# Two rows of w3 loaded ahead of k, a pairwise maximum for batch 0, and a new order for the first third of the list

## The chip, the cores and the metric

The kernel runs on one core of a Trainium2 chip. The metric is device time in microseconds of one launch; for the kernel before it is 227.48 us, the median of 3 runs (227.4 to 227.79).

## The reference

There are eight batches of 8 heads, 576 positions and 64 features. From q, k and v a linear attention is computed, and its output goes through a feed-forward block with a product in place of an activation:

```
q_s = exp(q - max over features); q_s /= sum + 1e-9
k_s = exp(k - max over positions); k_s /= sum + 1e-9
kv  = k_s^T v           (64 x 64 for each head)
x   = q_s kv            (4608 tokens x 512)
out = ((x w1) * (x w2)) w3 w_out
```

Inputs and output are float32; w1 and w2 are 512 x 1024, w3 is 1024 x 1024, w_out 1024 x 512.

## The kernel before, in words

Since nothing nonlinear stands between w3 and w_out, the kernel first multiplies them on chip to one matrix W3O (1024 x 512), and every token then goes through x w1, x w2, their product, and one multiplication with W3O.

**The fold** (`fold(ft)`, L384 to L412). For each of the eight rows ft of w3 (128 x 1024, cast to float16 by its load): `w3t.ft` transposes eight 128 x 128 blocks on TensorE into a bank of PSUM, `w3T.ft` copies them to SBUF (on ScalarE or VectorE, into one of two buffers), `pf.ft.0` and `pf.ft.1` multiply four blocks each with one half of w_out (`wo.0`, `wo.1`), and `W3O.ft` scales the sum into place.

**Attention** (`attention(b)`, from L417). For q: `qmx` maximum, `qsub` subtraction, `qexp` exponential, `qsm` sum, `qeps` and `qrc` its reciprocal, `qn` scaling. The result is transposed: by TensorE for batch 0 (`qt`, copied by `qT`), by a DMA for the others (`qd`). For k: the maximum over positions is taken in two steps, `kmx` over the nine positions that a partition holds, and `cb` across partitions (two transposes of 32 x 32 blocks and small reductions). Then `ksub` and `kexp`, `kv` (TensorE, k_s^T v), `kv2` (division by the sums), `xm` and `xt` (TensorE, x for 512 and the last 64 positions of the batch) and `xs`, `xts` (copies out of PSUM). For batch 0, k and q are loaded and worked on by pairs of heads (the last number in a name), and `kmx` is one reduction per pair (L426); for the other batches ScalarE copies two positions into PSUM (`kmi`, L433) and VectorE takes maxima of that bank with the rest in SBUF (`kmx_half`, L437).

**Chunks** (`chunk(c)`, from L795). Chunk c is the first 512 positions of batch c; chunk 8 collects the last 64 of all batches. `up.1` and `up.0` are x w2 and x w1 (L809), `bs` copies the first out of PSUM, `ab` is the product, `down` multiplies with W3O (L842), `os` copies out, `st` stores. Later chunks use a variant with fewer products (`um`, `dm` and their additions, with the sums of weights `ws` and `wt`).

**Order.** `ORDER` (L83) is a list of all steps, written out, and `Plan.run` (L52) emits them in this order. A letter behind a slash is the engine (`/A` ScalarE, `/D` VectorE, `/P` GpSimd). Each engine works off its own steps in the order of the list and waits at each for what it needs. The steps `zero.0` to `zero.6` (L302) multiply a tile of zeros and feed nothing; the number behind the slash is the count of 128 x 512 matmuls, and `zero.0` has 13.

**Loads.** q of batch 0 is loaded from SyncE; the weights, and k, v and the other q of batches 0 and 1, from GpSimd, whose queue also runs its own computing steps in the same order (L375). The loads of batches 2 to 7 come from SyncE, and those of batch 2 start when `w1.1` has landed (GATES, L80). VectorE and GpSimd steps marked `port` are made to run one after another where the engine changes (L69).

Of the kernel before, what the change touches and what calls it, by code (L numbers as in the profile page):

```python
# [10 lines left out]
F32 = mybir.dt.float32  # L11
F16 = mybir.dt.float16
AF = mybir.ActivationFunctionType
ALU = mybir.AluOpType
# [69 lines left out]
zero.5/3 zero.0 zero.1/1 q.0.0 qmx.0.0 qsub.0.0/D q.0.1 qmx.0.1 ident w3.3 w3.4 qexp.0.0 w3t.3 w3T.3/A qsm.0.0  # L84
qeps.0.0/D qsub.0.1/D zero.4/3 zero.2/1 w3t.4 zero.3/6 w3T.4/A wo.0 pf.3.0 pf.4.0 qexp.0.1 qrc.0.0 qn.0.0/D qt.0.0.0
qt.0.0.4 qT.0.0.4/A wo.1 pf.3.1 zero.6/1 qsm.0.1 w3.6 w3t.6 qeps.0.1/A qrc.0.1 qT.0.0.0/D qn.0.1/D pf.4.1 W3O.4/D w3.0
w3t.0 W3O.3/D w3T.6/A pf.6.0 qt.0.1.0 w3T.0/A qT.0.1.0/A qt.0.1.4 pf.6.1 qT.0.1.4/A W3O.6/A pf.0.0 k.0.1 kmx.0.1 k.0.0
w3.7 w3t.7 w3T.7/A pf.0.1 w3.5 w3t.5 pf.7.0 pf.7.1 w3T.5/A pf.5.0 w3.1 w3.2 v.0 k.1 kmx.0.0 cb.0 ksub.0.0/D kexp.0.0
w3t.1 w3T.1/D W3O.7/A ksub.0.1/D pf.5.1 w2.1 w2.0 w1.0 q.1.0 W3O.5/D w2.2 w3t.2 pf.1.0 kexp.0.1 pf.1.1 W3O.1/D w1.1
kv.0.0 kv.0 kv2.0 w3T.2/A pf.2.0 kmi.1 kmx.1.0 xm.0.1 xt.0 xs.0.1.1/A xs.0.1.0/A xts.0.0/A xts.0.1/D pf.2.1 W3O.2/A  # L90
xm.0.0 xs.0.0.1/A xs.0.0.0/A q.1.1 up.1.0.1.0 W3O.0/A wt.1/P up.1.0.1.1 up.1.0.0.1 up.1.0.0.0 bs.0.1.1/A up.0.0.0.0
bs.0.0.1/A kmx.1.1 cb.1 bs.0.0.0/A qmx.1.0 up.0.0.0.1 up.0.0.1.0 qsub.1.0/D ksub.1.1/D ab.0.0.1 qexp.1.0 qsm.1.0
up.1.0.0.3 bs.0.0.3/A up.0.0.1.1 ab.0.1.1 q.2 v.1 kexp.1.1 k.2 qeps.1.0/A ksub.1.0/P up.1.0.1.2 kexp.1.0 up.1.0.0.2
qrc.1.0 bs.0.0.2/A qn.1.0/P up.0.0.0.3 up.0.0.0.2 ab.0.0.0 qmx.1.1 qd.1.0 qsub.1.1/P bs.0.1.0/A ab.0.0.3 up.1.0.1.3
up.0.0.1.3 ab.0.0.2 k.3 ab.0.1.0 bs.0.1.3/A ab.0.1.3 ws.1.1/D up.0.0.1.2 bs.0.1.2/A ab.0.1.2 down.0.0.0 qmx.2.0
down.0.0 down.0.1.0 down.0.1 vc.1.1/A vc.1.0/A qexp.1.1 qsm.1.1 qeps.1.1/A ws.1.0/P qsub.2.0/P kv.1.0 kv.1 q.3 kv2.1
qexp.2.0 down.0.2.0 down.0.2 qrc.1.1 xm.1.0 qn.1.1/P qd.1.1 qmx.2.1 down.0.3.0 down.0.3 qsm.2.0 qeps.2.0/D kmi.2
kmx.2.0 qsub.2.1/P xs.1.0.0/A v.2 xs.1.0.1/A up.1.1.0.0 bs.1.0.0/A os.0.2/A st.0.2 up.0.1.0.0 os.0.3/A qrc.2.0
qn.2.0/P wt.2/P up.1.1.0.1 up.0.1.0.1 bs.1.0.1/A qexp.2.1 kmx.2.1 up.1.1.0.2 cb.2 bs.1.0.2/A ksub.2.0/P up.0.1.0.2
up.1.1.0.3 os.0.0/A os.0.1/A xm.1.1 xs.1.1.1/A qsm.2.1 xs.1.1.0/D ab.1.0.1 qeps.2.1/A qrc.2.1 ab.1.0.0 bs.1.0.3/A  # L100
up.0.1.0.3 up.1.1.1.0 up.0.1.1.0 up.1.1.1.1 qmx.3.1 up.0.1.1.1 ab.1.0.3 ab.1.0.2 bs.1.1.0/A up.1.1.1.2 up.0.1.1.2
up.1.1.1.3 qn.2.1/P kexp.2.0 down.1.0.0 down.1.0 kmi.3 kmx.3.0 bs.1.1.1/A ab.1.1.1 vc.2.0/A qd.2.0 xt.1 bs.1.1.2/A
ksub.2.1/P vc.2.1/A kmx.3.1 cbt.3 kexp.2.1 qsub.3.1/P xts.1.0/A ab.1.1.2 xts.1.1/A q.4 qexp.3.1 ws.2.0/P ab.1.1.0 kv.2
kv2.2 down.1.1.0 down.1.1 qd.2.1 xm.2.1 qmx.3.0 qsub.3.0/P os.1.0/A bs.1.1.3/A xs.2.1.1/A qmx.4.1 qsub.4.1/P xm.2.0
xs.2.0.1/A xt.2 qsm.3.1 xs.2.0.0/A xs.2.1.0/A cbx.3 xts.2.1/A v.3 down.1.2.0 up.0.1.1.3 up.1.2.0.0 bs.2.0.0/A qmx.4.0
xts.2.0/D up.0.2.0.0 up.1.2.0.1 qsub.4.0/P up.0.2.0.1 up.1.2.0.2 k.4 v.4 qexp.3.0 cb.3 ksub.3.1/P qsm.3.0 os.1.1/A
up.0.2.0.2 ab.1.1.3 up.1.2.0.3 q.5 qeps.3.1/A qrc.3.1 qn.3.1/P bs.2.0.1/A st.1.0 qexp.4.1 qsm.4.1 bs.2.0.2/A ab.2.0.2
ab.2.0.1 qexp.4.0 kmi.4 up.0.2.0.3 up.1.2.0.4 up.0.2.0.4 qeps.3.0/A kmx.4.0 qrc.3.0 vc.3.1/A bs.2.0.3/A ab.2.0.3
qn.3.0/P ab.2.0.0 bs.2.0.4/A kexp.3.1 up.1.2.0.5 up.0.2.0.5 q.6 qsm.4.0 bs.2.0.5/A ab.2.0.5 up.1.2.0.6 qeps.4.1/A
st.0.3 qd.3.1 kmx.4.1 down.1.2 qrc.4.1 ab.2.0.4 down.1.3.0 up.0.2.0.6 up.1.2.0.7 up.0.2.0.7 qd.3.0 os.1.2/A down.1.3  # L110
bs.2.0.6/A qmx.5.0 ab.2.0.6 vc.3.0/A ksub.3.0/P kexp.3.0 st.1.2 qeps.4.0/A bs.2.0.7/A qn.4.1/P os.1.3/A qsub.5.0/P
qrc.4.0 qn.4.0/P cbt.4 cbx.4 kv.3 ab.2.0.7 qexp.5.0 down.2.0 kv2.3 xm.3.0 xs.3.0.1/A xs.3.0.0/A xm.3.1 xs.3.1.0/A xt.3
xts.3.1/A xts.3.0/A cb.4 ksub.4.1/P k.5 qmx.6.1 down.2.1 xs.3.1.1/D qsm.5.0 vc.4.1/A os.2.1/A ksub.4.0/P up.1.3.0.0
up.0.3.0.0 qmx.6.0 qsub.6.0/P bs.3.0.0/A ab.3.0.0 os.2.0/A qeps.5.0/A qrc.5.0 st.1.1 qmx.5.1 qsub.5.1/P up.1.3.0.1
up.0.3.0.1 up.1.3.0.2 up.0.3.0.2 bs.3.0.1/A qd.4.1 up.1.3.0.3 up.0.3.0.3 up.1.3.0.4 ab.3.0.1 v.5 kmi.5 kmx.5.0 kmx.5.1
cbt.5 st.2.1 kexp.4.0 vc.4.0/A kexp.4.1 kv.4 bs.3.0.2/A qsub.6.1/P kv2.4 bs.3.0.4/A up.0.3.0.4 ab.3.0.4 down.2.2
bs.3.0.3/A ab.3.0.2 qexp.5.1 qd.4.0 cbx.5 qsm.5.1 qexp.6.0 xm.4.1 xs.4.1.0/A xm.4.0 xs.4.0.1/A qn.5.0/P xs.4.0.0/A
up.1.3.0.5 ws.3.1/D up.0.3.0.5 up.1.3.0.6 up.0.3.0.6 v.6 qeps.5.1/A wt.4/D ws.4.0/D os.2.2/A wt.3/D ws.3.0/D qrc.5.1
qn.5.1/P qexp.6.1 cb.5 ksub.5.0/P bs.3.0.6/A ab.3.0.6 k.6 vc.5.0/A xs.4.1.1/A up.1.3.0.7 up.0.3.0.7 q.7 qsm.6.1
ab.3.0.3 bs.3.0.5/A vc.6.0/A up.1.4.0.0 ab.3.0.5 up.0.4.0.0 up.1.4.0.1 st.1.3 bs.3.0.7/A ksub.5.1/P up.0.4.0.1 qsm.6.0  # L120
kmi.6 bs.4.0.1/A bs.4.0.0/A kmx.6.0 st.2.0 vc.6.1/A down.2.3 qeps.6.1/A os.2.3/A qrc.6.1 kmx.6.1 up.1.4.0.2 qd.5.0
qn.6.1/P qeps.6.0/A qrc.6.0 qn.6.0/P up.0.4.0.2 ab.4.0.0 up.1.4.0.3 bs.4.0.2/A ab.4.0.2 up.0.4.0.3 up.1.4.0.4
up.0.4.0.4 cbt.6 kexp.5.0 bs.4.0.3/A vc.5.1/A qmx.7.0 qsub.7.0/P ab.4.0.3 cbx.6 up.1.4.0.5 ab.4.0.1 cb.6 up.0.4.0.5
ksub.6.1/P bs.4.0.4/A ab.4.0.4 ab.3.0.7 st.0.0 xt.4 kexp.5.1 kv.5 xts.4.0/A qexp.7.0 kv2.5 bs.4.0.5/A ab.4.0.5 dm.3.1
xts.4.1/D dm.3.2 de.3.1/A qd.5.1 xm.5.0 xm.5.1 xs.5.0.1/A xs.5.0.0/A qd.6.0 ad.3.1/D xs.5.1.0/A up.1.4.0.6 up.0.4.0.6
up.1.4.0.7 up.0.4.0.7 xs.5.1.1/A st.0.1 ksub.6.0/D kexp.6.0 ad.3.3/D bs.4.0.6/A dm.3.7 kexp.6.1 bs.4.0.7/A ws.2.1/D
ad.3.2/D dm.3.6 xd.5.3/D de.3.7/A ab.4.0.6 xt.5 ad.3.4/P qmx.7.1 ab.4.0.7 xts.5.1/D kv.6 xts.5.0/A dm.3.4 de.3.2/A
dm.3.5 de.3.4/A kv2.6 dc.3.3 qd.6.1 xm.6.1 xs.6.1.0/A qsub.7.1/P dc.3.1 xd.5.2/P xs.6.1.1/A qsm.7.0 um.5.2.1 um.5.1.1
ue.5.1.1/A ue.5.2.1/A xm.6.0 xd.5.4/D xt.6 xts.6.0/A ad.4.1/D dm.3.3 xts.6.1/A dc.3.2/A um.5.1.6 xd.5.1/D dc.3.4/D
ue.5.1.2/A k.7 xs.6.0.1/A ad.4.2/D um.5.2.6 ue.5.2.2/A ad.4.4/D um.5.1.7 ws.4.1/D um.5.2.7 ue.5.2.7/A um.5.0.7  # L130
um.5.1.5 ue.5.1.4/A ue.5.1.7/A ad.4.3/D um.5.2.2 uc.5.2.1 qeps.7.0/A um.5.0.1 xs.6.0.0/A um.5.2.4 uc.5.2.3 qrc.7.0
ue.5.0.7/A um.5.1.3 uc.5.1.4/P ab.5.1.1 ue.5.0.1/A um.5.2.5 ue.5.2.4/A um.5.1.2 uc.5.1.1 ab.5.2.0/P st.3.0 st.2.2
um.5.0.2 uc.5.0.1 um.5.0.4 um.5.0.6 ue.5.0.2/A uc.5.0.3 uc.5.2.4/P um.5.3.7 xd.6.3/P qn.7.0/P dm.4.1 kmi.7 kmx.7.0
um.5.3.1 ue.5.3.7/A um.5.1.4 uc.5.1.3 ab.5.1.0/P kmx.7.1 ue.5.3.1/A um.5.3.2 uc.5.3.1 de.4.1/A um.5.0.5 ue.5.0.4/A
uc.5.0.4/P um.5.3.6 xd.6.2/P ue.5.3.2/A dm.4.6 um.5.2.3 ab.5.2.1 um.6.0.1 qexp.7.1 qsm.7.1 cbt.7 um.5.3.5 ue.5.3.4/A
dm.4.2 xd.6.1/D dm.4.7 um.6.2.1 um.5.0.3 um.5.3.3 dc.4.1 ab.5.0.1 v.7 vc.7.1/A um.5.3.4 uc.5.3.3 uc.5.3.4/P ab.5.0.0/P
de.4.7/A dm.4.4 st.3.1 qeps.7.1/A qrc.7.1 ue.6.0.1/A ab.5.3.1 um.6.0.6 ab.5.3.0/P um.6.0.7 cbx.7 cb.7 de.4.2/A dc.4.3
xd.6.4/D ue.6.0.2/A ue.6.0.7/A ue.6.2.1/A dm.4.5 de.4.4/A dc.4.4/D um.6.0.5 ue.6.0.4/A uc.6.0.4/D st.4.1 um.6.1.1
ue.6.1.1/A um.6.2.7 ue.6.2.7/A dm.4.3 dc.4.2/A um.6.3.1 ue.6.3.1/A um.6.0.4 um.6.3.7 ue.6.3.7/A um.6.0.2 ksub.7.1/D
ksub.7.0/D qd.7.0 qn.7.1/P kexp.7.1 um.6.1.6 um.6.3.6 um.6.2.6 ue.6.2.2/A uc.6.0.3 uc.6.0.1 ab.6.0.0/P um.6.3.4  # L140
vc.7.0/A um.6.2.4 uc.6.2.3 um.6.0.3 ab.6.0.1 um.6.2.2 uc.6.2.1 um.6.1.2 uc.6.1.1 um.6.1.7 um.6.3.2 uc.6.3.1 ab.6.2.0/P
# [25 lines left out]
def kernel(  # L167
# [11 lines left out]
    nc = tc.nc  # L179
    B, H, S, D = q.shape  # L180
# [81 lines left out]
    OWN = (3, 384)  # L262
    LAST = [0, 256, 384, 512]
    FEXP = []
    CX = [3, 4, 5, 6, 7]
    DH = [0, 1]
    KE = []
    ABX = []
# [108 lines left out]
    for b in range(2, B):  # L377
        for n in "kqv":
            load((n, b), "SP")
# [803 lines left out]
```

## Time and profile before

| what | value |
|---|---|
| median of 3 runs | 227.48 us |
| the profiled execution | 227.57 us |
| its span in the profile | 225.8 us |
| TensorE busy | 219.3 us, 97% |
| VectorE busy | 203.9 us, 90% |
| ScalarE busy | 161.6 us, 72% |
| GpSimd busy | 141.1 us, 62% |

The span is the profiler's time from first to last instruction; the execution's own time is 1.8 us longer. Busy time is the union of an engine's instructions. TensorE's matmuls are pipelined with modelled ends, so the rate is better read from starts: 16 matmuls of 512 columns start within 3.5 us. In the views a row gives start, duration, engine, line, operation and tiles; what stands in brackets is the idle time just before and what ended it.

### The profile page before, as it was taken

To read this page: it belongs to the slowest core of one execution; us is meant where nothing else is said; L and a number is where in the kernel's file an instruction comes from. 1 tells how busy PE (TensorE), PEld (TensorE's weight loads), DVE (VectorE), ACT (ScalarE), POOL (GpSimd) and SP (SyncE) were. 2 spreads that over 40 slices of the span, in tenths; PEclk is the share of its full clock that TensorE was granted. 3 is DMA by queue.
4 is the path that set the end of the run, shared out by engine and by line. 5 is a ranking of instruction groups with operands and counts; after the bars stand their busy time and mean duration, and the time that the engine had idled before them with its cause. 6 is when DMAs were issued, how large, how long until landed. Compare 5 with 4: busy or idle time off the path is not lost.

```text
span 225.8 us, 5662 instructions
## 1 busy us (share of the span) xinstructions
PE 219.3 (97%) x2250; PEld 150.6 (67%) x2250; DVE 203.9 (90%) x363; ACT 161.6 (72%) x280; POOL 141.1 (62%) x96
## 2 busy tenths in 40 slices
PE   7998999999999999999999999999999999999994
PEld 2454658865886544444444657888888888888853
DVE  2989879989998999999998999999999988899881
ACT  2556476785859997899999986988995846453511
POOL 8344405787999799999679928297474055602320
PEclk9999999999999999999999999999999999999999
DMA  6999999999999999999969186482193040044343
GB/s 222 214 273 248 294 227 251 367 387 300 277 276 369 388 324 357 187 312 280 385 164 296 22 134 212 128 221 96 32 200 64 3 107 34 3 124 157 89 145 139
DMA packets 38042, 46.89 MB, mean 208 GB/s; under 512 B 18048, under 2 KB 21504, under 8 KB 38016
## 3 DMA queue, kind: packets, MB, share of 16 engines
q1 hardware_dynamic: 32144, 35.92, 56.5%
q0 software_dynamic: 5728, 10.55, 20.0%
q8 instruction: 17, 0.28, 0.5%
q10 hardware_dynamic: 144, 0.07, 0.1%
q14 instruction: 9, 0.07, 0.1%
HBM read 38.80 MB, written 9.44 MB: 214 GB/s over the span
## 4 chain that ended last, share of the span: by engine, by line
PE 67%; DMA 20%; DVE 8%; ACT 2%; POOL 1%; issue 1%; POOLq 0%; ACTq 0%; SPq 0%; DVEq 0%
PE pab L809 19%; PE uA L904 12%; PE dA L945 8%; DMA w1sb<-in_moe_w_dram 8%; PE uB L904 6%; PE po L842 6%; DMA w<-in_moe_w_dram 5%; DMA wosb<-in_moe_w_out_dram 5%; PE dB L945 4%; DMA q<-in_q_dram 3%; PE uC L904 3%; PE po L857 3%; PE dC L945 2%; DVE qm L547 2%; PE pkv L501 2%; DVE qr L579 2%
## 5 line engine op out<-in xcount | busy, mean ns | idle before, releaser
L809 PE MATMUL pab<-x,w2sb 128*128 128x256 f16 (+1 forms) x224 | 40.6, 318 | 0.0
L809 PE MATMUL pab<-x,w1sb 128*128 128x256 f16 (+1 forms) x224 | 40.6, 318 | 0.0
L597 POOL TENSOR_TENSOR en<-eq,qr 128x1024 f16<-128x1024 f16 (+1 forms) x14 | 29.7, 2126 | 8.3 <-DVE k L475 4.3
L809 PEld LDWEIGHTS <-w2sb 128*128 128x128 f16 x224 | 21.6, 98 | 13.4 <-issue 1.0
L809 PEld LDWEIGHTS <-w1sb 128*128 128x128 f16 x224 | 21.7, 98 | 13.0 <-issue 0.2
L553 POOL TENSOR_TENSOR q<-q,qm 128x1280 f32<-128x1280 f32 (+1 forms) x13 | 27.7, 2143 | 2.2 <-DVE qm L547 1.8
L475 POOL TENSOR_TENSOR k<-k,cb 128x1152 f32<-128x1152 f32 x10 | 26.2, 2626 | 2.5 <-DVE k L475 2.5
L904 PEld LDWEIGHTS <-w 128*128 128x128 f16 x256 | 25.0, 98 | 3.3
L834 DVE TENSOR_TENSOR ab<-pab,bsb 128x512 f16<-128x512 f32 x40 | 25.9, 672 | 0.2
L275 ACT CAST bsb<-pab 128x512 f16<-128x512 f32 x40 | 23.2, 594 | 3.8 <-PE pab L809 3.6
L561 ACT ACTIVATE eq<-q 128x1024 f16<-128x1024 f32 (+2 forms) x16 | 18.7, 1169 | 8.2 <-DVE q L553 7.6
L547 DVE TENSOR_REDUCE qm<-q 128x16 f32<-128x1024 f32 (+2 forms) x16 | 21.2, 1333 | 3.7 <-DMA q<-in_q_dram 3.7
L842 PE MATMUL po<-W3O,ab 128*128 128x512 f16 x96 | 22.7, 380 | 0.0
L579 DVE TENSOR_REDUCE qr<-eq 128x16 f32<-128x1024 f16 (+2 forms) x16 | 21.4, 1339 | 0.0
L483 ACT ACTIVATE ek<-k 128x1152 f16<-128x1152 f32 x16 | 18.8, 1172 | 3.3 <-DVE k L475 2.4
L279 ACT ACTIVATE x<-xm 128x512 f16<-128x512 f32 x30 | 16.4, 605 | 3.6 <-PE xm L649 1.9
L904 PE MATMUL uA<-v,w 128*128 128x256 f16 x128 | 17.9, 273 | 0.0
L275 ACT COPY v<-uA 128x512 f32<-128x512 f32 x24 | 14.1, 601 | 4.8 <-PE uA L904 4.3
L945 PEld LDWEIGHTS <-k 128*128 128x128 f16 x160 | 15.5, 98 | 2.1
L883 POOL TENSOR_TENSOR k<-ab,k 128x1024 f16<-128x1024 f16 x3 | 6.4, 2130 | 16.4 <-DVE bsb L883 10.0
L275 ACT CAST v<-v 128x1152 f16<-128x1152 f32 x14 | 16.3, 1170 | 0.0
L398 PE MATMUL pf<-wosb,aux 128*128 128x512 f16 x64 | 15.6, 379 | 0.4 <-DMA wosb<-in_moe_w_out_dram 0.4
(140 smaller groups left out, 464.7 us busy)
## 6 DMA issues: line engine op xcount, KB each, us to landing
q<-in_q_dram SPq DMA_DIRECT2D x6, 1152.0 KB, 6.5
k<-in_k_dram SPq DMA_DIRECT2D x6, 1152.0 KB, 8.9
v<-in_v_dram SPq DMA_DIRECT2D x6, 1152.0 KB, 8.8
out_dram<-outs SPq DMA_DIRECT2D x23, 256.0 KB, 3.5
out_dram<-outs SPq DMA_DIRECT2D x25, 128.0 KB, 5.9
w<-in_moe_w_dram POOLq DMA_DIRECT2D x8, 256.0 KB, 11.4
q<-in_q_dram SPq DMA_DIRECT2D x2, 576.0 KB, 4.2
k<-in_k_dram POOLq DMA_DIRECT2D x2, 576.0 KB, 13.2
```

The source lines that it names most:

```text
L275: return [(nc.scalar.copy if eng == "ACT" else engine[eng].tensor_copy)(out=out, in_=in_)]
L475: return [engine[eng].tensor_tensor(out=kb[:, two(hp), :, :], in0=kb[:, two(hp), :, :], in1=st["cb", b][:, two(hp), None, :].broadcast_to( ...
L483: nc.scalar.activation(out=st["ek", b][:, hp, :, :].rearrange("p j (i d) -> p i j d", i=2), in_=kb[:, two(hp), :, :], func=AF.Exp)
L547: dve.tensor_reduce(out=st["qm", b][:, hs, j], in_=qb[:, hs, j, :], axis=AX.X, op=ALU.max, **({"negate": True} if (b, p) in FEXP else {}))
L553: return [engine[eng].tensor_tensor(out=qb[:, hs, j, :], in0=qb[:, hs, j, :], in1=st["qm", b][:, hs, j, None].broadcast_to([P, nh, n, D]), ...
L579: dve.tensor_reduce(out=st["qr", b][(slice(None), *part(p))], in_=st["eq", b, p], axis=AX.X, op=ALU.add)
L597: return [engine[eng].tensor_tensor(out=st["en", b][:, j, hs, :].rearrange("p j h d -> p h j d"), in0=st["eq", b, p], in1=st["qr", b][:, h ...
L809: nc.tensor.matmul(st["p", one, c, sub, u][:, a * (t1 - t0):(a + 1) * (t1 - t0)], lhsT=w[:, ct, fb * P:(fb + 1) * P], rhs=x()[:, ct, t0:t1 ...
L834: dve.tensor_tensor(out=st["ab", c][:, nf * u:nf * u + nf, t0:t1], in0=cut(st["p", 0, c, sub, u]), in1=cut(st["bsb", c, sub, u]), op=ALU.mult)
L842: nc.tensor.matmul(st["po", c, tb], lhsT=st["ab", c][:, ft, tb * P:(tb + 1) * P], rhs=W3O[:, ft, :], start=(ft == 0), stop=(ft == N_FT - 1))
L904: nc.tensor.matmul(t[:, u, :], lhsT=w[:, k0 + kk, fb * P:(fb + 1) * P], rhs=r[:, kk, :], start=(p in (1, 2, 7) and u == 0 and kk == 0), st ...
L945: nc.tensor.matmul(t[:, i, :], lhsT=l[:, f, i * P:(i + 1) * P], rhs=r[:, f, :], start=(p in (1, 2, 7) and i == 0 and f == 0), stop=(i == 1 ...
```

## The change

Three things are changed.

1. Two more rows of w3 (w3.7 and w3.5) stand ahead of k of batch 0 in GpSimd's queue. Before: w3.3 w3.4 wo.0 wo.1 w3.6 w3.0 k.0.1 k.0.0 w3.7 w3.5 w3.1 w3.2 v.0. After: w3.3 w3.4 wo.0 wo.1 w3.6 w3.0 w3.7 w3.5 k.0.1 k.0.0 w3.1 w3.2 v.0, with qsub.0.1 between w3.7 and w3.5 and qn.0.1, qn.0.0 around v.0.
2. The maximum of batch 0 is taken as for the other batches, but by pairs of heads: `kmi_one` copies two positions of two heads into PSUM on ScalarE, `kmx_max` takes five maxima on VectorE.
3. The first 353 steps of the list (up to `os.1.2`) are ordered anew, some on other engines. Of the seven zero steps, four move from the start of the list to places among the chunks of batches 0 to 2; the counts stay. `ALOAD` is empty and changes nothing.

The list, cut to its first steps and the lines that hold zero steps; then the code:

```diff
-zero.5/3 zero.0 zero.1/1 q.0.0 qmx.0.0 qsub.0.0/D q.0.1 qmx.0.1 ident w3.3 w3.4 qexp.0.0 w3t.3 w3T.3/A qsm.0.0
-qeps.0.0/D qsub.0.1/D zero.4/3 zero.2/1 w3t.4 zero.3/6 w3T.4/A wo.0 pf.3.0 pf.4.0 qexp.0.1 qrc.0.0 qn.0.0/D qt.0.0.0
-qt.0.0.4 qT.0.0.4/A wo.1 pf.3.1 zero.6/1 qsm.0.1 w3.6 w3t.6 qeps.0.1/A qrc.0.1 qT.0.0.0/D qn.0.1/D pf.4.1 W3O.4/D w3.0
-w3t.0 W3O.3/D w3T.6/A pf.6.0 qt.0.1.0 w3T.0/A qT.0.1.0/A qt.0.1.4 pf.6.1 qT.0.1.4/A W3O.6/A pf.0.0 k.0.1 kmx.0.1 k.0.0
-w3.7 w3t.7 w3T.7/A pf.0.1 w3.5 w3t.5 pf.7.0 pf.7.1 w3T.5/A pf.5.0 w3.1 w3.2 v.0 k.1 kmx.0.0 cb.0 ksub.0.0/D kexp.0.0
-w3t.1 w3T.1/D W3O.7/A ksub.0.1/D pf.5.1 w2.1 w2.0 w1.0 q.1.0 W3O.5/D w2.2 w3t.2 pf.1.0 kexp.0.1 pf.1.1 W3O.1/D w1.1
...
+zero.5/3 zero.0 zero.1/1 q.0.0 qmx.0.0 qsub.0.0/D q.0.1 qmx.0.1 ident w3.3 w3.4 qexp.0.0 w3t.3 w3T.3/A wo.0 wo.1 w3.6
+w3.0 w3.7 w3t.4 w3T.4/D qsub.0.1/P w3.5 k.0.1 k.0.0 w3.1 pf.3.0 qexp.0.1 qsm.0.1 pf.4.0 pf.4.1 qeps.0.1/D w3.2 qsm.0.0
+qrc.0.1 W3O.4/A w3t.6 pf.3.1 qeps.0.0/D w3T.6/D kmi.0.1 pf.6.0 w3t.7 kmi.0.0 pf.6.1 w3t.5 qrc.0.0 w3T.7/D pf.7.0
+pf.7.1 qn.0.1/P qt.0.1.0 w3T.5/D kmx.0.1 kmx.0.0 v.0 w3t.0 w3T.0/A qn.0.0/P pf.5.0 pf.5.1 qt.0.0.4 W3O.7/A qT.0.0.4/A
+pf.0.0 w3t.2 w3T.2/A k.1 qt.0.1.4 w2.1 w2.0 w1.0 cb.0 ksub.0.0/D W3O.3/A pf.0.1 qt.0.0.0 W3O.0/A pf.2.0 pf.2.1
+ksub.0.1/D kexp.0.0 w3t.1 qT.0.1.0/D W3O.6/D kexp.0.1 kv.0.0 kv.0 W3O.2/D w3T.1/D pf.1.0 kv2.0 qT.0.1.4/A W3O.5/D
+kmi.1 kmx.1.0 qT.0.0.0/A xm.0.0 xs.0.0.0/A xs.0.0.1/A xm.0.1 xt.0 xs.0.1.1/A xts.0.0/D xs.0.1.0/A pf.1.1 W3O.1/D
+kmx.1.1 up.1.0.0.0 up.1.0.0.1 up.1.0.1.1 up.0.0.1.1 q.1.0 w2.2 bs.0.0.1/A w1.1 q.2 q.1.1 up.1.0.1.0 v.1 wt.1/P
+bs.0.1.0/A xts.0.1/A bs.0.0.0/A qmx.1.0 qsub.1.0/P qexp.1.0 up.0.0.0.0 cb.1 ksub.1.1/D bs.0.1.1/A kexp.1.1 qsm.1.0
...
+ab.0.0.2 ab.0.0.3 qsub.1.1/P ab.0.1.0 zero.2/1 up.0.0.1.3 ab.0.1.3 up.0.0.1.2 ab.0.1.2 ws.1.1/P vc.1.1/A down.0.0.0
...
+up.0.1.0.2 os.0.3/A qsm.2.0 qeps.2.0/A vc.2.1/A kmx.2.1 zero.6/1 bs.1.0.1/A qrc.2.0 up.1.1.0.3 cb.2 qexp.2.1 vc.2.0/A
...
+zero.4/3 qmx.3.0 ws.2.0/P up.0.1.1.2 xts.1.0/A qmx.4.0 xm.2.1 xs.2.1.0/A st.0.2 xm.2.0 xs.2.0.1/A cbt.3 xs.2.0.0/A
...
+ab.2.0.5 kmx.4.1 zero.3/6 bs.2.0.4/A down.1.2 q.6 qrc.4.1 ab.2.0.4 down.1.3.0 up.0.2.0.6 up.1.2.0.7 up.0.2.0.7 qd.3.0
...
+    KM = [0]
+    ALOAD = []
...
+        def kmi_one(hp):
+            st["kmp", b, hp] = bank([P, 2, 2, D], F32, "kmp")
+            nc.scalar.copy(out=st["kmp", b, hp], in_=kb[:, two(hp), 0:2, :].rearrange("p h j d -> p j h d"))
+
+        def kmx_max(hp):
+            t = st["kmp", b, hp]
+            top = lambda out, in0, in1: dve.tensor_tensor(out=out, in0=in0, in1=in1, op=ALU.max)
+            for j in (2, 4, 6):
+                top(t, t, kb[:, two(hp), j:j + 2, :].rearrange("p h j d -> p j h d"))
+            if ("km", b) not in st:
+                st["km", b] = work.tile([P, HH, D], F32, tag="km", name="km")
+            m = st["km", b][:, two(hp), :]
+            top(m, t[:, 0], kb[:, two(hp), 8, :])
+            top(m, t[:, 1], m)
...
-                A(("kmx", b, hp), "DVE", lambda hp=hp: kmx_one(hp), [("k", b, hp)])
+                if b in KM:
+                    A(("kmi", b, hp), "ACT", lambda hp=hp: kmi_one(hp), [("k", b, hp)], takes="ps", kind="kmi1")
+                    A(("kmx", b, hp), "DVE", lambda hp=hp: kmx_max(hp), [("kmi", b, hp)], gives=[("kmi", b, hp)],
+                      kind="kmq")
+                else:
+                    A(("kmx", b, hp), "DVE", lambda hp=hp: kmx_one(hp), [("k", b, hp)])
```

## The prediction on record

> **What bounds the kernel now.** The page first (busy time by engine), then TensorE's waits, then its share of two long stages, then the chain of work that ended last.
>
> ```profile
> span 225.8 us, 5662 instructions
> ...
> PE 219.3 (97%) x2250; PEld 150.6 (67%) x2250; DVE 203.9 (90%) x363; ACT 161.6 (72%) x280; POOL 141.1 (62%) x96
> ```
> ```profile
> PE zero L306 <- DVE zero L300: 1.6, 1, 1.6
> PE w3t L388 <- DMA w<-in_moe_w_dram: 1.0, 2, 0.9
> PE pf L398 <- DMA wosb<-in_moe_w_out_dram: 0.4, 1, 0.4
> PE xm L649 <- DMA qT<-en: 0.3, 1, 0.3
> ```
> ```profile
> 33.70:76.40 42.70, 42.32 (x490) 31.43 (x487) 40.09 (x76) 32.25 (x51) 34.64 (x17) 1.00 1.12 323
> 76.40:222.70 146.30, 146.30 (x1461) 103.15 (x1458) 137.16 (x246) 111.15 (x206) 92.00 (x53) 1.00 0.61 167
> ...
> 219.22 3.51 PE po L857 x32
> ```
>
> TensorE (PE) is the bound. All its waits on others sum to 3.3 us, and after 33.7 us only one of 0.3 us is seen; in the second stage it is busy 146.30 of 146.30. A busy row can hide gaps, since ends are modelled, so I also look at starts. VectorE (DVE) is full as well (137 of 146), but no wait of PE names it: it is just in time. So the end is set by one sum: the PE work left when the opening is over. A change gains only by taking waiting or filler out of the opening, and any matmul put behind it is paid.
>
> The opening is a matter of loads and fillers:
>
> ```profile
> 1.55 5.95 PE L306 MATMUL zero<-zero 128*128 128x512 f16 x17 [1.55 <-DVE zero L300]
> 7.42 0.71 PE L388 MATMUL w3t<-ident,w 128*128 128x128 f16 x8
> 7.97 1.03 PE L306 MATMUL zero<-zero 128*128 128x512 f16 x4
> 8.83 0.66 PE L388 MATMUL w3t<-ident,w 128*128 128x128 f16 x8
> 9.33 1.46 PE L306 MATMUL zero<-zero 128*128 128x512 f16 x6
> 11.19 1.89 PE L398 MATMUL pf<-wosb,aux 128*128 128x512 f16 x8 [0.41 <-DMA wosb<-in_moe_w_out_dram]
> ...
> 14.41 0.38 PE L306 MATMUL zero<-zero 128*128 128x512 f16 x1
> ...
> 20.19 0.72 PE L388 MATMUL w3t<-ident,w 128*128 128x128 f16 x8 [0.18 <-DMA w<-in_moe_w_dram]
> 20.75 1.03 PE L398 MATMUL pf<-wosb,aux 128*128 128x512 f16 x4
> ...
> 29.43 0.48 PE L501 MATMUL pkv<-v,ek 64*64 64x64 f16 x36
> ...
> 31.84 0.56 PE L649 MATMUL xm<-qT,kv 64*64 64x256 f16 x8
> ...
> 33.70 3.67 PE L809 MATMUL pab<-x,w2sb 128*128 128x256 f16 x32
> ```
>
> The columns are start, time, what. Zero matmuls fill the waits: 17 ahead of the first row of w3, then 4 + 6 + 1 = 11 more in gaps before 14.5 us. The chunk work (L809) starts at 33.70.
>
> **The change, step by step.**
>
> *The fillers.* Both lists hold the same seven zero steps with the same counts (28 matmuls). Before, all are done by 14.6 us. After, 17 stay ahead of w3t.3; `zero.2/1`, `zero.6/1`, `zero.4/3`, `zero.3/6`, 11 matmuls, stand among the chunks of batches 0 to 2, where PE has no wait to fill. Price of one: the run of six lasts 0.43 longer than the run of four (1.46 against 1.03), 0.215 each. 11 x 0.215 = **+2.4 us** in the full stage. Bounds: 0 if each stands in a wait that the new order brings anyway (the wait is then the price), 2.4 in full. I take 2.4, by the row 146.30 of 146.30. Taking the 11 out of the opening gains nothing by itself: their gaps end when data land.
>
> *The loads.* Loads of the software queue are issued by GpSimd (POOL):
>
> ```profile
> 7.67 0.55 POOL L358 DMA_DIRECT2D w<-in_moe_w_dram  x1 [1.41 <-DMA w<-in_moe_w_dram]
> ...
> 17.82 0.74 POOL L358 DMA_DIRECT2D w2sb<-in_moe_w_dram  x1 [0.73 <-DMA k<-in_k_dram]
> 19.30 0.74 POOL L358 DMA_DIRECT2D w2sb<-in_moe_w_dram  x1 [0.73 <-DMA k<-in_k_dram]
> 20.43 0.74 POOL L358 DMA_DIRECT2D w1sb<-in_moe_w_dram  x1 [0.39 <-DMA w<-in_moe_w_dram]
> 22.86 0.76 POOL L358 DMA_DIRECT2D q<-in_q_dram  x1 [1.70 <-DMA w<-in_moe_w_dram]
> ...
> 25.05 0.74 POOL L358 DMA_DIRECT2D w1sb<-in_moe_w_dram  x1 [0.51 <-DMA w<-in_moe_w_dram]
> 27.96 0.76 POOL L358 DMA_DIRECT2D q<-in_q_dram  x1 [2.17 <-DMA v<-in_v_dram]
> ```
>
> The ninth issue (7.67) waits for the first load, and so on: each later issue tells when the load eight places earlier landed, in the order issued. Before: k.0.1 about 17.7, k.0.0 19.2, w3.7 20.2, w3.5 22.6, w3.2 24.8, v.0 27.9. After, w3.7 and w3.5 stand ahead of k. From k.0.0 to w3.2 four such rows take 5.6 us, between 1.0 (w3.7) and 2.4 (w3.5). A k piece takes 1.5, so w3.0 lands at 16.2. With 1.3 for a row (1.0 and 1.4, the mean, are its bounds): w3.7 17.5, w3.5 18.8, k.0.1 20.2, k.0.0 21.7; the bytes ahead of w3.1, w3.2 and v.0 are as before, so these land as before. POOL now also does `qsub.0.1` after the seventh issue and `qn.0.1`, `qn.0.0` around v.0, and the issues queue behind them:
>
> ```profile
> 7.14 1.35 DVE L547 TENSOR_REDUCE qm<-q 128x18 f32<-128x1152 f32 x1
> 41.08 2.62 POOL L475 TENSOR_TENSOR k<-k,cb 128x1152 f32<-128x1152 f32 x1 [2.49 <-DVE k L475]
> 43.66 1.90 POOL L597 TENSOR_TENSOR en<-eq,qr 128x1024 f16<-128x1024 f16 x1
> ```
>
> `qsub.0.1` waits for `qmx.0.1` (the L547 row, over at 8.5) and takes 2.6: w3.5 is issued near 11.1, the two k by 13.2, while wo.1 (wo.0 lands only at 11.2), w3.6, w3.0 and w3.7 are still in flight. The two `qn` (1.90 x 1152/1024 = 2.1 each) put v.0's issue at about 17.5 and k.1's at 20.3; their turns come at 24.8 and 27.9. So I cost these at nothing, covered by the loads in flight; without that cover v.0 would be late by as much as its issue moved, 2.4 us.
>
> *PE's opening after.* Halves of pf are 4 matmuls, 0.86; w3t is 0.55 (20.19 to 20.75). It waits 8.0 to 8.8 and 9.4 to 11.2 for w3.4 and wo.0, and shortly for wo.1, w3.6 and w3.7 (17.5). Then it has work: w3t.7 and pf.6.1 to 18.9, w3t.5 19.5, pf.7 21.2, w3t.0 and the first qt 22.0, pf.5 23.7, qt and pf.0.0 24.9, w3t.2 25.4, qt, pf.0.1, qt 26.8, pf.2 28.5, w3t.1 29.1. Then kv.0.0, with 8 pf matmuls left. Before, kv.0.0 started at 29.43, also with 8 left. **No gain**: the two waits for w3 (1.0 us in the table of waits, w3t.7 and w3t.5) come back as the gaps that fillers used to hold.
>
> *The k chain* lands later and feeds kv:
>
> ```profile
> 17.67 4.27 DVE L429 TENSOR_REDUCE km<-k 128x128 f32<-128x1152 f32 x2
> ...
> 24.28 1.36 DVE L475 TENSOR_TENSOR k<-k,cb 128x1152 f32<-128x1152 f32 x1
> ...
> 33.18 0.28 DVE L281 TENSOR_SCALAR xtail<-xt 128x128 f16<-128x128 f32 x1
> ...
> 34.10 0.42 DVE L439 TENSOR_TENSOR km<-kmp,k 128x256 f32<-128x256 f32 x1
> ```
> ```profile
> 28.53 1.17 ACT L483 ACTIVATE ek<-k 128x1152 f16<-128x1152 f32 x1 [1.20 <-DVE k L475]
> ...
> 30.64 0.59 ACT L435 COPY kmp<-k 128x512 f32<-128x512 f32 x1
> ```
>
> The pairwise maximum is three operations on 128x256 (0.42 each, 0.46 with the gap) and two on 128x128 (bounds 0.2 and 0.42; I take the 0.28): 1.9 against 2.14 for one reduce, and a copy on ScalarE (ACT) of half of that 0.59 row's size (0.3 to 0.59; I take 0.4). So k.0.1 at 20.2, copy 20.6, kmx.0.1 22.5, kmx.0.0 (k.0.0's copy at 22.1) 24.4, cb 2.3 (21.94 to 24.28) 26.7, two ksub 29.4, kexp.0.1 (1.17) 30.6, against 29.7 before. kv.0 then runs from 30.6 to about 31.4 (36 products in 0.48, and short ones). DVE has qT, W3O.6, W3O.2 and w3T.1 behind ksub (some 2.3 by the nearest rows, 0.28 to 0.7 each), so pf.1.0 starts at 31.7 and ends 32.6; two xm and xt, 0.9 by the xm row, 33.5; pf.1.1 34.3. **Chunk work starts at 34.3 instead of 33.70: +0.6 us.** ACT waits for k in its copies, with w3T.0 queued behind; pf.0.0 needs that at 24.0 and gets it near 23.1, so 0.9 us of cover.
>
> *Moved between engines.* ACT gives DVE four w3T copies; DVE gives POOL two qn, qsub.0.1, qsub.1.0 and ws.1.1, which are as long or longer: DVE has less to do, POOL some 10.6 us more (2.6, two of 2.1, two near 1.9). PE waits for neither now (no row of its waits names them behind 1.6 us), so I cost this at nothing; if POOL's `qsub`, `ksub` and `qn` of batch 1 come late by the 1.9 of a `ws`, xm.1 waits that long, a part of the upper end.
>
> *Sum.* 2.4 + 0.6 = +3.0 us on the profiled execution's 227.57 (span 225.8 and 1.8 around it), 230.6; that run lies 0.1 over the median 227.48, so **230.5**. From `os.1.2` on the lists agree; nothing there can give it back.
>
> **A rule weighed.** Fillers may also hold the pace.
>
> ```profile
> 1.96 0.15 PEld L306 LDWEIGHTS <-zero 128*128 128x128 f16 x1 [0.28 <-issue]
> ...
> 5.80 1.21 PEld L306 LDWEIGHTS <-zero 128*128 128x128 f16 x6 [0.28 <-issue]
> ```
>
> From 1.96 to 5.80 nine fillers start 0.43 apart, then 0.215 apart: after its idle start PE ran at half pace for about 4.2 us. After the change it has, from 7.42 to 11.2, only 16 transposes. The Trainium skill, "TensorE: Matmul & The Clock Gate", Part 1, says that an idle window of about 3.4 us brings the half clock back, and Part 4 that transposes do not count as work for it; by that rule the pf matmuls from 11.2 on could run at half pace. No row of this trace has such a gap.
>
> **Rivals.**
> - *Half pace again* (chance 0.17): ten matmuls at 0.215 extra, 2.1 us, of which the short waits before 17.5 take back some 1.0; with the k chain or ACT's copies later by up to 1 us too: +1 to +3 on the forecast, 232.3. For it: the gap of 3.8 us; against: it isn't wholly idle. PE would show 512-wide matmuls 0.43 apart after 11.2.
> - *Fillers partly in waits* (0.15): the new order's fillers cover the 0.3 at 62.4 and hidden gaps, and the opening loses its 1.0 us: with 0.6 for the two in the middle, 2.4 + 0.6 - 1.6 = +1.4, 228.9.
> - *No difference* (0.05): the same with the k chain as early as before (-0.6) and shorter gaps ahead of wo.0 and wo.1 (-0.7, their landing that much earlier): 227.6.
> - *Faster* (0.04): one mechanism, an earlier start of the chunks: k lands no later, because loads in flight share the queue instead of standing in line, and chunk work begins as soon as w2.1 is there:
>
> ```profile
> w2sb<-in_moe_w_dram POOLq DMA_DIRECT2D x2, 256.0 KB, 13.9
> ```
>
> 17.82 + 13.9 = 31.7, 2.0 us ahead of 33.70; with the waits of the middle covered (0.9 by estimate) that is 2.4 - 2.9 = -0.5, 227.0. It decides where chunks begin before about 31.3 with the fillers paid in full. Against it: landings in the order of issue.
> - *The loads don't move* (0.02, in the first rival's range): w3.5's issue, held on POOL, lands after k.
>
> **How the numbers follow.** Forecast 0.57, own range 229.4 to 231.5 (k's landing +-0.5, the opening +-0.5, new stalls). The 8-in-10 range takes in the partly covered fillers and most of the half-pace case: 228.4 to 232.6. This kernel's runs tell 0.2% (0.45 us) from no change: faster 0.04, same 0.06, slower 0.90.
>
> **What would show it.** Right: 17 fillers before 7.4 us and 11 after 43; PE idle about 2.5 us before 11.2; w3t.7 near 17.5; L809 first at 34.3; PE busy without waits from there, its end 3 us later. Wrong: L809 starting before 32.5, fillers in the middle with waits around them, k.0 landing before 19.5, or wo.0 landing before 11.

## The result, and the profile after

| | before | after |
|---|---|---|
| median | 227.44 us (227.28 to 227.79, 4 runs) | 229.81 us (229.32 to 230.19, 4 runs) |
| the profiled execution | 227.57 | 229.6 |
| its span | 225.8 | 227.8 |

The changed kernel is slower by 1%: the ratio is 1.0098, with a 95% interval of 1.0076 to 1.012. The forecast was 230.5 (228.4 to 232.6).

Line numbers are shifted by the new code: by 2 at first (L398 is L400 now), later by 17 (L501 is L518, L649 is L666) and 22 (L809 is L831, L842 is L864); in the runs of the experiments by at most one line less. Busy times first, from the page of after:

```profile
span 227.8 us, 5676 instructions
...
PE 219.4 (96%) x2250; PEld 151.1 (66%) x2250; DVE 200.4 (88%) x369; ACT 158.8 (70%) x279; POOL 151.5 (66%) x101
```

TensorE (PE) has the same 2250 matmuls and the same busy time, in a span that is 2.0 us longer. VectorE lost 3.5 us of work, GpSimd got 10.4 more, and neither is felt. What PE waits for, in the table of waits of after (total, times, longest):

```profile
PE pf L400 <- DMA wosb<-in_moe_w_out_dram: 1.7, 1, 1.7
PE zero L308 <- DVE zero L302: 1.6, 1, 1.6
PE w3t L390 <- DMA w<-in_moe_w_dram: 1.3, 2, 0.8
PE pkv L518 <- ACT ek L500: 0.3, 1, 0.3
```

The waits for loads that fillers used to hold are in the open now (1.7 and 1.3 against 0.4 and 1.0). These two rows sum to 1.6 us more, but the chunk work starts only 0.61 later, so most of that was made up for in the opening. The timeline of PE in after (start, duration, what, and in brackets the idle time ahead):

```profile
1.55 5.17 PE L308 MATMUL zero<-zero 128*128 128x512 f16 x17 [1.55 <-DVE zero L302]
7.54 0.71 PE L390 MATMUL w3t<-ident,w 128*128 128x128 f16 x8 [0.81 <-DMA w<-in_moe_w_dram]
8.77 0.70 PE L390 MATMUL w3t<-ident,w 128*128 128x128 f16 x8 [0.53 <-DMA w<-in_moe_w_dram]
11.21 4.38 PE L400 MATMUL pf<-wosb,aux 128*128 128x512 f16 x12 [1.73 <-DMA wosb<-in_moe_w_out_dram]
...
17.73 0.66 PE L390 MATMUL w3t<-ident,w 128*128 128x128 f16 x8
...
29.56 0.21 PE L518 MATMUL pkv<-v,ek 64*64 64x64 f16 x1 [0.28 <-ACT ek L500]
...
34.31 2.78 PE L831 MATMUL pab<-x,w2sb 128*128 128x256 f16 x24
...
46.54 0.38 PE L308 MATMUL zero<-zero 128*128 128x512 f16 x1
...
61.91 0.38 PE L308 MATMUL zero<-zero 128*128 128x512 f16 x1
...
73.02 0.81 PE L308 MATMUL zero<-zero 128*128 128x512 f16 x3
...
89.10 1.46 PE L308 MATMUL zero<-zero 128*128 128x512 f16 x6
...
221.09 3.66 PE L879 MATMUL po<-W3O,ab 128*128 128x512 f16 x32
```

Three numbers of this list carry the rest. The chunk work starts at 34.31 (33.70 before); 11 fillers stand behind it; the last matmul ends at 221.09 + 3.66 = 224.75 (219.22 + 3.51 = 222.73 before). From the first chunk matmul to the last matmul it is 190.44 us, against 189.03 before. I call this stretch **the middle**. Without its 11 fillers (11 x 0.215 = 2.37) the middle of after is 188.07, so 0.95 shorter than the one before. The whole difference of the two executions is therefore

0.61 (later start) + 2.37 (fillers) - 0.95 (shorter middle) = 2.03 us = 229.6 - 227.57.

The 0.95 was not in the prediction. In the timeline of before it shows as PE starting late without being counted as idle (four rows, two of them neighbours each time):

```profile
61.12 1.04 PE L809 MATMUL pab<-x,w2sb 128*128 128x256 f16 x8
62.42 0.41 PE L649 MATMUL xm<-qT,kv 64*64 64x256 f16 x8 [0.27 <-DMA qT<-en]
...
71.59 0.26 PE L649 MATMUL xt<-qT,kv 64*64 64x64 f16 x8
71.67 1.18 PE L501 MATMUL pkv<-v,ek 64*64 64x65 f16 x72
```

Eight matmuls of 256 columns start over 0.87 us (the next eight follow after that much), so xm could have begun at 61.99 and begins at 62.42; and the 72 products of kv.2 take 1.18 where the same group takes 0.78 at 51.23. Those are 0.8 of the 0.95. In after both are gone: kv.2 takes 0.78 there, at 71.36, and xm begins 0.96 behind the first of the eight matmuls ahead of it, in place of 1.30.

### The profile page after: what moved, and what is told of

It reads as the page before. It is cut to its first block, busy times and chain, and to the rows that moved or that the text cites. A ratio compares the mean times of both kernels' runs of the same rounds, so it can differ in the third digit from the quotient of the medians.

```text
span 227.8 us, 5676 instructions
## 1 busy us (share of the span) xinstructions
PE 219.4 (96%) x2250; PEld 151.1 (66%) x2250; DVE 200.4 (88%) x369; ACT 158.8 (70%) x279; POOL 151.5 (66%) x101
## 4 chain that ended last, share of the span: by engine, by line
PE 85%; DVE 6%; DMA 6%; POOL 1%; issue 0%; ACT 0%; DVEq 0%
PE pab L831 31%; PE uA L926 12%; PE po L864 9%; PE dA L967 8%; PE uB L926 6%; DMA k<-in_k_dram 4%; PE dB L967 4%; PE uC L926 3%; PE po L879 3%; PE pkv L518 2%; PE xm L666 2%; PE dC L967 2%; DMA q<-in_q_dram 2%; DVE kmp L445 1%; DVE qm L564 1%; DVE k L492 1%
## 5 line engine op out<-in xcount | busy, mean ns | idle before, releaser
L831 PE MATMUL pab<-x,w2sb 128*128 128x256 f16 (+1 forms) x224 | 40.8, 318 | 0.0
L831 PE MATMUL pab<-x,w1sb 128*128 128x256 f16 (+1 forms) x224 | 40.8, 318 | 0.0
L614 POOL TENSOR_TENSOR en<-eq,qr 128x1024 f16<-128x1024 f16 (+2 forms) x16 | 34.0, 2127 | 9.7 <-DVE mxe L478 4.5
L570 POOL TENSOR_TENSOR q<-q,qm 128x1024 f32<-128x1024 f32 (+2 forms) x15 | 31.7, 2127 | 4.5 <-DVE qm L564 4.4
L831 PEld LDWEIGHTS <-w2sb 128*128 128x128 f16 x224 | 21.6, 98 | 13.7 <-issue 0.8
L831 PEld LDWEIGHTS <-w1sb 128*128 128x128 f16 x224 | 21.8, 98 | 13.1 <-issue 0.2
L864 PE MATMUL po<-W3O,ab 128*128 128x512 f16 x96 | 22.7, 379 | 0.0
L400 PE MATMUL pf<-wosb,aux 128*128 128x512 f16 x64 | 17.2, 410 | 1.9 <-DMA wosb<-in_moe_w_out_dram 1.7
L277 ACT COPY v<-uA 128x512 f32<-128x512 f32 x24 | 14.1, 601 | 4.8 <-PE uA L926 4.3
```

The source lines that it names most:

```text
L277: return [(nc.scalar.copy if eng == "ACT" else engine[eng].tensor_copy)(out=out, in_=in_)]
L570: return [engine[eng].tensor_tensor(out=qb[:, hs, j, :], in0=qb[:, hs, j, :], in1=st["qm", b][:, hs, j, None].broadcast_to([P, nh, n, D]), ...
L614: return [engine[eng].tensor_tensor(out=st["en", b][:, j, hs, :].rearrange("p j h d -> p h j d"), in0=st["eq", b, p], in1=st["qr", b][:, h ...
L831: nc.tensor.matmul(st["p", one, c, sub, u][:, a * (t1 - t0):(a + 1) * (t1 - t0)], lhsT=w[:, ct, fb * P:(fb + 1) * P], rhs=x()[:, ct, t0:t1 ...
L864: nc.tensor.matmul(st["po", c, tb], lhsT=st["ab", c][:, ft, tb * P:(tb + 1) * P], rhs=W3O[:, ft, :], start=(ft == 0), stop=(ft == N_FT - 1))
```

## The experiments

Each was run against the kernel before on the same chip (its median there 227.44 to 227.55). "Start" and "middle" are read in the one profiled execution of a kernel, which need not be its median one (those of a1 and a3 are the slowest of their twelve); fillers behind the start are taken out of the middle at 0.215 each.

| run | what | median, us (runs) | ratio to before, 95% interval | profiled | start | middle |
|---|---|---|---|---|---|---|
| before | | 227.44 | | 227.57 | 33.70 | 189.03 |
| after | | 229.81 (4) | 1.0098 [1.0076, 1.0120] | 229.60 | 34.31 | 188.07 |
| a1_fill_back | after, fillers back in the opening | 227.37 (12) | 0.9997 [0.9982, 1.0013] | 228.75 | 35.85 | 188.07 |
| a2_fill_drop | after, the four steps left out | 228.28 (12) | 1.0037 [1.0021, 1.0053] | 228.23 | 34.21 | 189.17 |
| a3_late_one | after, one matmul in each late step | 228.05 (12) | 1.0030 [1.0012, 1.0048] | 229.87 | 36.11 | 188.07 |
| b1_fill_late | before, fillers late | 230.48 (4) | 1.0129 [1.0113, 1.0145] | 230.51 | 33.95 | 189.36 |
| b2_fill_drop | before, the four steps left out | 228.40 (12) | 1.0039 [1.0027, 1.0050] | 228.26 | 33.64 | 189.76 |
| c1_reduce | a1 with the one reduction | 227.61 (12) | 1.0003 [0.9987, 1.0020] | 227.78 | 34.65 | 188.28 |
| c2_kfirst | a1 with k first | 230.87 (4) | 1.0149 [1.0132, 1.0167] | 230.88 | 37.97 | 188.06 |
| h1_one_row | a1, w3.5 behind k | 228.15 (11) | 1.0033 [1.0022, 1.0045] | 228.60 | 35.71 | 188.06 |
| d1_open_before | opening of before, rest of after | 227.84 (11) | 1.0010 [0.9996, 1.0025] | 227.84 | 34.90 | 188.07 |
| d2_open_after | opening of after, rest of before | 228.87 (11) | 1.0074 [1.0050, 1.0098] | | | |
| d3_open_before | d1, seam mended | 227.09 (10) | 0.9981 [0.9966, 0.9995] | 226.94 | 33.27 | 188.82 |
| d4_fill_one | a1, one matmul in each filler step | 227.39 (12) | 0.9993 [0.9979, 1.0007] | 227.30 | 34.16 | 188.27 |

Theory: a late filler is paid in full. Rivals: it stands in waits that are there anyway, or its absence from the opening costs the pace of PE.

**Fillers back (a1), left out (a2).**

```diff
-w3t.3 w3T.3/A wo.0 ... w3t.4 w3T.4/D ... pf.4.0 pf.4.1
+w3t.3 zero.4/3 zero.2/1 w3T.3/A wo.0 ... w3t.4 zero.3/6 w3T.4/D ... pf.4.0 zero.6/1 pf.4.1
-ab.0.1.0 zero.2/1 up.0.0.1.3 ... kmx.2.1 zero.6/1 bs.1.0.1/A ... wt.2/P zero.4/3 qmx.3.0 ... kmx.4.1 zero.3/6 bs.2.0.4/A
+ab.0.1.0 up.0.0.1.3 ... kmx.2.1 bs.1.0.1/A ... wt.2/P qmx.3.0 ... kmx.4.1 bs.2.0.4/A
```

> The changed kernel with its four late zero steps (11 matmuls) put back into the opening: 4 behind w3t.3, 6 behind w3t.4, 1 ahead of pf.4.1. Theory (late fillers are paid in full, the half pace after 11.2 us is absorbed by the wait for k): 2.0 to 2.4 us less than the changed kernel, about 227.5; the pf matmuls after 11.2 us start 0.215 apart, and yet chunk work still starts at 34.2 to 34.4, because kexp.0.0 sets it. Rival A (the late fillers covered the 0.95 us of waits that the changed kernel lacks in the middle): only 1.4 less, 228.4. Rival B (the half pace is part of the loss): chunk work starts 1 us or more earlier and the time falls by over 3 us, under 226.8.

> The changed kernel with its four late zero steps left out altogether (17 fillers are left of 28; they feed nothing, so the result stays whole). Theory: the same time as with the fillers put back, within 0.3 us, about 227.5, with the half pace after 11.2 us still there and chunk work at 34.3. Rival B (the half pace costs): 1 us or more slower than with the fillers put back.

a1 took 227.37: 2.44 less than after, for 11 matmuls that by rate take 2.37. Its middle, which holds no filler, is the 188.07 that is left of after's when the 2.37 are taken out. So the fillers are the whole loss; the rest of the change, its later start and its shorter middle, cancels to nothing that can be told from before. a2 missed: 228.28, 0.9 over a1. Its opening is not the cause, since its chunk work starts at 34.21; its middle is 1.1 longer than a1's. In its timeline ScalarE (ACT) waits for v of batch 7, and PE then for ACT:

```profile
155.88 1.16 ACT L276 CAST v<-v 128x1152 f16<-128x1152 f32 x1 [1.58 <-DMA v<-in_v_dram]
157.57 1.03 PE L967 MATMUL dB<-aux,ab 128*128 128x256 f16 x8 [0.45 <-ACT q L276]
159.71 1.03 PE L967 MATMUL dA<-aux,k 128*128 128x256 f16 x8 [0.23 <-ACT q L276]
```

That load was issued at 145.13 and took 10.7 us; in before, after and a1 ACT begins on its data 9.1 us behind the issue without waiting for it, so there it took 9.1 at most. The two waits of PE are 0.68 of the 1.1. The four dropped steps stand 110 us ahead of it or more.

**The same on the kernel before (b1, b2).**

```diff
-w3t.3 w3T.3/A ... zero.4/3 zero.2/1 w3t.4 zero.3/6 w3T.4/A ... pf.3.1 zero.6/1 qsm.0.1
+w3t.3 w3T.3/A ... w3t.4 w3T.4/A ... pf.3.1 qsm.0.1
```

b1 has them again ahead of up.0.0.1.3, up.1.1.0.3, up.0.1.1.2 and down.1.2; b2 has them nowhere.

> The kernel before with nothing changed but its four zero steps, moved from the opening to the places that they have in the changed list (ahead of up.0.0.1.3, up.1.1.0.3, up.0.1.1.2 and down.1.2). Theory: 11 x 0.215 = 2.4 us more behind the start of the chunks, less up to 0.8 where one of them covers a wait of the middle (0.43 ahead of xm.1.1, 0.4 at kv.2), and 0 to 0.8 more at the start from the half pace, which the two waits for w3 (1.0 us) mostly take back: 229.2 to 230.2. Rival (the loss of the change is the later k, not the fillers): under 228.2.

> The kernel before with the same four zero steps left out (17 fillers are left). It shows by itself what the fillers of the opening are worth. Theory: half pace from 11.2 us on for some 8 matmuls, 1.7 us, of which the waits for w3.7 and w3.5 (1.0 us and hidden ones) take most: 0 to 0.8 slower than before, 227.4 to 228.3. Rival (the fillers of the opening hold the pace and that is what the change loses): 1.5 us or more slower.

b1: 230.48, 3.0 over before, where 1.7 to 2.7 were expected: 2.37 of fillers, 0.25 of a later start and 0.3 in the middle. Together the late fillers covered no wait. The 0.3 has its place at kv.2, where before loses 0.4 and b1 waits (PE's timeline in b1):

```profile
73.45 1.06 PE L500 MATMUL pkv<-v,ek 64*64 64x65 f16 x71 [0.62 <-DVE km L438]
```

b2: 228.40, 0.1 over the range and 0.9 over before, with the same late v of batch 7 (ACT waits 1.1 for it).

**One matmul in each late step (a3)**, `zero.4/3` to `zero.4/1` and `zero.3/6` to `zero.3/1` in after.

> The changed kernel with its four late zero steps at one matmul each, 4 in place of 11, at the same places. Theory (each late filler is paid in full): 7 x 0.215 = 1.5 us less than the changed kernel's 229.8, so 228.3, within 0.4. Rival (the three behind up.1.1.1.2 or the six ahead of down.1.2 stand in waits): less than 0.8 us off, over 229.0.

228.05, 0.7 over a1 and 1.8 under after, for 4 matmuls (0.86) instead of 11: the price goes by the count of matmuls, not by the count of places. (The profiled execution, 229.87, met the half clock twice, as the last section shows for a1.)

**One matmul in each, at the early places (d4)**, the same edit in a1.

> The kernel after with its four late filler steps back at their places in the opening but with one matmul in each instead of 3, 1, 6 and 1 (4 instead of 11), so that the number of PSUM tiles stays and only the filler work shrinks. With all 11 there the time was 227.4, with the four steps and their tiles left out 228.3, by 0.9 of which no part lay in the opening. If the tiles' places decide: 227.4 (227.1 to 227.7). If the filler work decides: 228.0 to 228.5.

227.39, as a1. Seven filler matmuls less in the opening change nothing, but leaving out the four steps with their four PSUM tiles costs 0.9 (a2), and a like amount in b2. So the loss does not go by the count of filler matmuls. Whether the tiles bring it or the last four matmuls is not shown, as no run keeps the tiles without a matmul; and how either, near 10 us, makes a load of 145 us land some 1.6 us later was not found, and stays open.

**The maximum as one reduction (c1)**: a1 with `KM = []` and without `kmi.0.1`, `kmi.0.0`.

> The changed kernel with its fillers put back into the opening, and the maximum of batch 0 taken again by one reduction for each pair of heads, without the two copies into PSUM: the pairwise maximum alone is undone. Theory: no difference, 227.4 within 0.3, since the reductions (2.14 each) start when k.0.1 lands, 0.4 earlier than the first maximum behind its copy, and end at about 24.5 as now. Rival (the shorter maximum shortens the k chain): chunk work starts 0.4 to 0.6 later and the time is 0.5 more.

227.61, no difference. The pairwise form in after (ACT and VectorE, timeline):

```profile
20.19 0.38 ACT L441 COPY kmp<-k 128x256 f32<-128x256 f32 x1 [3.97 <-DMA k<-in_k_dram]
21.70 0.38 ACT L441 COPY kmp<-k 128x256 f32<-128x256 f32 x1 [1.13 <-DMA k<-in_k_dram]
...
22.53 1.36 DVE L445 TENSOR_TENSOR kmp<-kmp,k 128x256 f32<-128x256 f32 x3
23.92 0.29 DVE L445 TENSOR_TENSOR km<-kmp,k 128x128 f32<-128x128 f32 x1
24.25 0.29 DVE L445 TENSOR_TENSOR km<-kmp,km 128x128 f32<-128x128 f32 x1
```

Five operations from 22.53 to 24.54, 2.0 us, against 2.14 for the reduction: nothing to gain, and a copy on ACT ahead. The profiled execution of c1 does start its chunk work 0.34 later than after, as the rival had it; but its copies of w3.7 and w3.5 begin some 0.3 later than a1's as well (18.61 and 19.97 against 18.30 and 19.65), so that start does not decide, and the time shows no loss.

**k ahead of w3.7 and w3.5 again (c2)**, and only w3.7 ahead of it, with the order on PE changed to suit (h1).

```diff
-w3.0 w3.7 w3t.4 ... qsub.0.1/P w3.5 k.0.1 k.0.0 w3.1
+w3.0 k.0.1 k.0.0 w3.7 w3t.4 ... qsub.0.1/P w3.5 w3.1        (c2)
+w3.0 w3.7 w3t.4 ... qsub.0.1/P k.0.1 k.0.0 w3.5 w3.1        (h1: pf.0 early, row 5 behind the maxima)
```

> The changed kernel with its fillers put back into the opening, and only the loads in the old order: k.0.1 and k.0.0 ahead of w3.7 and w3.5. Theory: TensorE, which takes w3t.7 and w3t.5 early in this order, waits for them until 20.2 and 22.6, and the maxima wait on VectorE behind the copies of these rows; chunk work starts near 37 in place of 34.3, 229.6 to 230.4. Rival (k's earlier landing makes up for it): under 228.4.

> The changed kernel with its fillers put back into the opening and only one of the two rows (w3.7) ahead of k; w3t.0 and pf.0 are taken ahead of pf.7, w3t.5 and pf.5 behind the maxima, w3T.5 is copied by ScalarE. Theory (the k chain sets the start of the chunks): k lands 1.3 us earlier, the chunks start at 32.9 to 33.5 in place of 34.3, and with TensorE full from there the time is 226.2 to 226.8. Rival (TensorE's work sets the start, not k): chunks at 34 and 227.4.

c2: 230.87, the direction as expected, the size 0.5 over. PE's timeline in c2:

```profile
20.44 0.71 PE L389 MATMUL w3t<-ident,w 128*128 128x128 f16 x8 [2.80 <-DMA w<-in_moe_w_dram]
20.99 1.77 PE L399 MATMUL pf<-wosb,aux 128*128 128x512 f16 x4
...
37.97 2.24 PE L830 MATMUL pab<-x,w2sb 128*128 128x256 f16 x19
```

In after the same w3t starts at 17.73: 2.7 later, and behind a wait of 2.80 the next four pf take 1.77 instead of 1.03. h1 was a failed guess: I took k for what sets the start of the chunk work and expected 226.2 to 226.8; it gave 228.15, with the start at 35.71, since PE now waits for the copies of w3T (waits of h1):

```profile
PE pf L399 <- ACT aux L276: 1.5, 2, 0.8
PE w3t L389 <- DMA w<-in_moe_w_dram: 0.8, 2, 0.5
```

In this order of the list TensorE is best served with both rows ahead of k: in c2 it waits for the row, in h1 for the copies that PE's changed order asks for earlier. One order with one row ahead was tried, so another may do better.

**Whose is the shorter middle? (d1, d2, d3)** d1 takes every step ahead of the first `up` from the list of before (its fillers and its reduction with them), and all others in the order and with the engines of after; d2 the reverse, with the fillers as in a1. The seam is the place where the two lists meet. d3 is d1 with its seam mended:

```diff
-W3O.0/A kmx.1.1 up.1.0.0.0 up.1.0.0.1 up.1.0.1.1 up.0.0.1.1 bs.0.0.1/A q.2 up.1.0.1.0
+W3O.0/A kmx.1.1 up.1.0.1.0 up.1.0.1.1 up.1.0.0.0 up.1.0.0.1 up.0.0.1.1 bs.0.0.1/A q.2
```

> Up to the first chunk matmul the list, the engines and the reduce of the kernel before (its fillers there too, no filler behind it); from there the order and engines of the kernel after. Theory (the time is a sum of three terms, the start of the chunk work, the PE work behind it, and the fillers behind it): chunk work starts near 33.7 as before, the middle takes 188.1 as in the runs with the new order and no filler (against 189.0 before), so the time is 227.45 - 0.9 = 226.5 (226.1 to 226.9), faster than both kernels. Rival (the shorter middle is a consequence of the new opening, whose loads of q, k and v of batch 1 are asked for at other times): the middle stays at 189.0 and the time is 227.5 (227.2 to 227.8), or more where the seam brings a wait.

> The other half: up to the first chunk matmul the list and engines of the kernel after, with the four fillers at their old places in the opening, then the order and engines of the kernel before. Theory (three terms): chunk work starts 34.3 to 34.7 (35.9 where the second stretch at half pace comes up), the middle takes 189.0 as before, so the time is 227.45 + 0.6 to 1.0 = 228.1 to 228.5. Rival (the opening brings the shorter middle): 188.1 from the same start, 227.1 to 227.5.

> The run with the opening of before and the rest of after, with its seam mended: there TensorE stood 1.45 us ahead of the first chunk matmul (34.90), because the rest of after begins with the first half of the columns of x, which the opening of before evicts last; here two steps on the other half (up.1.0.1.0 and up.1.0.1.1, 8 matmuls each, some 1.7 us together) stand first, as in the kernel before. Theory: chunk work starts at 33.5 to 33.7, the middle takes 188.1 as in the unmended run, so the profiled run ends 1.2 to 1.4 us earlier than its 227.84, and the time is 226.4 to 226.9: faster than both kernels. Rival (chunk work that starts earlier meets something else that is late behind it, q, k or v of batch 1): the middle is longer by what the start is earlier, 227.4 to 227.9.

d1: the middle was 188.07, as the theory had it, but at the seam PE stood 1.45 us for a half of x that the old opening evicts last:

```profile
34.90 2.78 PE L830 MATMUL pab<-x,w2sb 128*128 128x256 f16 x24 [1.45 <-ACT x L280]
```

so the time was 227.84, in the rival's range. d2: 228.87, 0.4 over the theory's range and far from the rival's 227.1 to 227.5. (Its profiled execution took 233.25, and no start and middle are read from it.) Of its other ten, six with a mean granted clock of 0.999 or more took 228.38 to 228.87, and four with 0.993 took 229.88 to 230.48; the latter fit the second stretch at half pace that the expectation names. Both runs say that the shorter middle belongs to the order behind the opening. d3: 227.09, between the theory's 226.4 to 226.9 and the rival's 227.4 to 227.9. PE's timeline in d3:

```profile
33.27 3.67 PE L830 MATMUL pab<-x,w2sb 128*128 128x256 f16 x32
...
53.74 0.52 PE L665 MATMUL xm<-qT,kv 64*64 64x256 f16 x8 [0.33 <-DVE kv L547]
54.19 1.90 PE L863 MATMUL po<-W3O,ab 128*128 128x512 f16 x8
56.13 1.03 PE L830 MATMUL pab<-x,w2sb 128*128 128x256 f16 x8
...
218.43 3.66 PE L878 MATMUL po<-W3O,ab 128*128 128x512 f16 x32
```

The chunk work starts 1.63 earlier than in d1, and 0.75 of that is given back: 0.33 at xm.1 (the division of kv by its sums, on VectorE, is not done), 0.2 ahead of 56.13 (eight matmuls of 512 columns start over 1.73, and here 1.94 pass), and small gaps. Each theory was half right. Six runs with the order of after (after, a1, a3, c2, h1 and d1) agree on a middle of 188.06 or 188.07 at starts from 34.31 to 37.97, which is what PE's work alone would give. At earlier starts batch 1's own chain is late, and it is just in time near 34.5: c1 (34.65) and d4 (34.16) have 188.28 and 188.27, with 1.87 and 1.93 in place of that 1.73. In after a filler at 46.54 stands ahead of this place. Some 0.2 of the fillers' 2.37 may thus stand in a delay that would be there without them; a1, which starts at 35.85, can't show that. d3 is the fastest of all, 0.2% under before (ratio 0.9981, interval 0.9966 to 0.9995), just more than the measurement can tell.

## Why the prediction was right, point by point

- *The fillers*, +2.4: right. a1 (2.44), a3 (1.76 for seven, where 1.5 was expected) and the decomposition (2.37) agree, and "fillers partly in waits" is refuted at its price of 1.6, though some 0.2 of that kind remains possible: that 229.81 lies on its side of the forecast is due to the middle, not to the fillers.
- *The loads*, k.0.1 at 20.2, k.0.0 at 21.7, w3.7 at 17.5: right. The copies that wait for k start at 20.19 and 21.70, w3t.7 at 17.73.
- *The k chain*, +0.6: right, 34.31. The maxima ended at 24.54 (24.4 forecast), and the last steps ahead of the chunk work came within 0.1 of it (pf.1.0 at 31.76 for 31.7, pf.1.1 at 33.44 for 33.5). That the start hangs on this chain alone is too simple: h1 shows that ACT's copies of w3T stand right beside it.
- *PE's opening, no gain*: right. kv.0.0 starts at 29.56 (29.1 forecast, 29.43 before). Between 6.7 and 11.2 PE stood idle for 3.1 us, where 2.5 was expected.
- *Moved between engines and new order of the middle*, costed at nothing: **this step failed, by its size.** It is worth -0.95 us. I had seen the 0.27 of a wait at 62.4 and put it into a rival as an "estimate of 0.9 in the middle" together with hidden gaps, yet into the forecast I took zero. With that term the sum is 230.5 - 0.95 = 229.55, against the measured 229.81. It is also why PE's work ended 2.0 us later and not 3.
- *The other rivals*: chunk work did not start before 31.3 ("faster"), and w3t.5 runs at 19.09, ahead of k ("the loads don't move").
- *The half pace* came in the profiled execution, as the weighed rule said, but not at the rival's price. The windows of after (span of time; busy time and counts of PE, PEld, DVE, ACT, POOL; granted clock; DMA share; GB/s):

```profile
34.31:77.00 42.69, 42.69 (x494) 31.89 (x493) 40.00 (x77) 32.24 (x52) 38.27 (x18) 1.00 1.11 313
77.00:224.75 147.75, 147.75 (x1464) 103.46 (x1462) 136.99 (x244) 110.90 (x206) 91.62 (x53) 1.00 0.62 166
11.00:13.00 2.00, 1.79 (x5) 0.69 (x5) 1.27 (x1) 0.69 (x1) 2.00 (x4) 0.53 1.05 208
13.00:15.00 2.00, 2.00 (x8) 0.68 (x7) 1.72 (x5) 0.00 (x0) 0.60 (x3) 0.62 1.09 205
```

The granted clock is 0.53 and 0.62 from 11 to 15 us and 1.00 from the start of the chunk work to the end. Where the fillers stand in the gap (a1, in the last section) it is 1.00 in both early windows. But the chunk work starts 14.12 us behind the copy of k.0.1 with the half pace (after, 20.19 to 34.31) and 14.13 behind it without (d4, 20.03 to 34.16): the lost time lies ahead of the waits for k, and they swallow it. The other executions say the same: over a whole execution the mean granted clock was 0.993 in the profiled one of after (229.60) and 1.000 in the three others (229.32, 230.02, 230.19), so three of four did not meet this stretch at all, and they were no faster. The rival named the right mechanism and saw only a part of its cover, the short waits before 17.5.

## What to carry to other kernels

Where one engine is full from some point on, a kernel's time is the moment at which that point is reached, plus the engine's work behind it, plus what filler is put there: read the three apart, and check the second in starts, since a busy share can hide waiting (before, in the first stage of its chunk work, showed 0.4 us idle where the starts show 0.8 lost). A filler is worth its place only where the engine would wait anyway. And a stage that starts earlier gains only until the next chain is late: of d3's 1.63 us, 0.75 went to batch 1.

## What the runs showed of the hardware

A gap with two runs of transposes in it was enough to bring the half clock back, in some executions. In after's profiled one, ahead of 11.21 us PE had been without 512-wide work since 1.55 + 5.17 = 6.72, so for 4.5 us, and had run sixteen transposes in that time; the loads of weights then stand 0.43 us apart instead of 0.215 (PEld in after):

```profile
11.59 0.15 PEld L400 LDWEIGHTS <-aux 128*128 128x128 f16 x1 [0.28 <-issue]
12.01 0.15 PEld L400 LDWEIGHTS <-aux 128*128 128x128 f16 x1 [0.28 <-issue]
12.44 0.15 PEld L400 LDWEIGHTS <-aux 128*128 128x128 f16 x1 [0.28 <-issue]
```

The Trainium skill, "TensorE: Matmul & The Clock Gate", Part 4, says that transposes do not count as work for the clock. This trace fits that, as no single wait in the gap is longer than 1.73 us; but no run replaces the transposes, so it is not shown. The same gap is shorter in b2, which has no fillers in it either: its 17 fillers last until 1.55 + 5.99 = 7.54, so it is 3.95 us (PE's timeline in b2, then a window, with the granted clock third from the end).

```profile
1.55 5.99 PE L305 MATMUL zero<-zero 128*128 128x512 f16 x17 [1.55 <-DVE zero L299]
...
11.49 1.89 PE L398 MATMUL pf<-wosb,aux 128*128 128x512 f16 x8 [1.73 <-DMA wosb<-in_moe_w_out_dram]
...
11.00:15.00 4.00, 3.41 (x21) 1.61 (x20) 3.11 (x5) 2.06 (x3) 1.06 (x2) 1.00 1.07 206
```

Here the clock stays at 1.00. By the same reading the gap is 3.2 us in b1 (1.00), and 4.2 and 4.5 in a2 and a3 (half clock). The recorded clock does not count the half pace at the start of an execution: it reads 1.00 from 1.5 to 5.8 us in before, where the fillers start 0.43 apart.

More surprising is a second stretch, it too in some executions only. The windows of a1's profiled execution (228.75; the other eleven 226.97 to 227.84):

```profile
11.00:13.00 2.00, 1.58 (x8) 0.78 (x9) 1.03 (x1) 0.94 (x1) 2.00 (x4) 1.00 1.03 204
13.00:15.00 2.00, 1.54 (x7) 0.41 (x5) 1.88 (x5) 0.19 (x1) 0.83 (x2) 1.00 1.13 212
28.00:31.00 3.00, 2.14 (x77) 1.57 (x78) 3.00 (x5) 2.48 (x3) 0.81 (x2) 1.00 1.32 242
31.00:35.00 4.00, 3.85 (x83) 2.05 (x84) 3.65 (x11) 2.10 (x5) 0.44 (x1) 0.60 1.22 262
```

From 31 to 35 us the clock is 0.60, right behind kv, where PE is busy 2.14 of 3 us, with eight transposes and products of 64 rows and 64 columns; the chunk work starts at 35.85, 15.58 behind the copy of k.0.1 (20.27) in place of 14.1. Here PE was never idle for longer than 0.59 us. Again there is a gap without 512-wide work, from the transposes at 28.39 to pf at 31.84, 3.45 us. In the profiled executions that met this stretch it is 3.45 (a1) and 3.19 (a3), in those that did not 3.13 (after) and 3.23 (d4), so its length alone does not decide. The Trainium skill, "TensorE: Matmul & The Clock Gate", Part 1, speaks of an idle window of about 3.4 us that runs on freely; a window that runs freely would explain why only some executions meet it, but what in it counts as idle no run here shows.
